# An attention and experts kernel: due times of its host-side planner set anew, and row slots copied by ScalarE block by block

## The chip, the cores and the metric

The kernel runs on one core of a Trainium2 chip. A core has five engines that run their own instruction streams: TensorE (PE; its weight loads are shown apart as PEld), VectorE (DVE), ScalarE (ACT), GpSimd (POOL) and SyncE (SP), which here issues most of the DMA transfers. The metric is the time of one execution on the device in microseconds. Times in the profile are of one profiled execution.

## The reference

Attention on queries that are averaged in twos, and then a layer of eight experts of which each token goes to its two best:

```python
# q, k, v: (4, 8, 1152, 64)
q_pool = q.reshape(B, H, S // 2, 2, D).mean(axis=3)          # 576 queries per head
scores = scale * np.matmul(q_pool, k.transpose(0, 1, 3, 2))
attn = np.exp(scores - scores.max(-1)); attn /= attn.sum(-1)
x = (attn @ v), heads side by side                           # 2304 tokens x 512
logits = x @ w_gate + log1p(exp(x @ w_noise)) * noise        # 8 experts
top2 of the logits, softmax over the two
for e in range(8): out[mask] += weight * (relu(x[mask] @ w1[e]) @ w2[e])   # 512 -> 1024 -> 512
```

## The kernel before

All products run on fp16 or bf16 parts: a float32 operand is split into a high part (ACT, `hi`, L303) and a remainder (DVE, `lo`, L300), and both are multiplied. The attention works through 16 *pairs* (two batch entries of one head), each of them loaded (`qr`, `kr`, `vr`), added in twos (`qs`, L472, on POOL or DVE), split into `qn`, `kn`, `vv`, and transposed by DMA into `qt`, `kt` (L306, issued by SP). For each pair a *maximum pass* of its own (L316 on PE, L324 on ACT, L328 and L346 on DVE) finds each query's largest score; `max_fin` (L353 to L355) writes the maxima into `qn2`, whose transpose `qt2` brings them into the scores. A *tile* of work is then: two chunks of scores on PE (L368, L369), one exponential on ACT (L376, 216 in all), the low half `pl` of the exponential (`p_lo`: one subtraction on DVE, L381, or two on POOL, L384), and the product with the values on PE (L404). Six buffers hold the exponentials, so `pf`, `pl` names repeat every six tiles.

After eight pairs the first half of the tokens is complete, and it is routed while the attention goes on with the other eight pairs: `steps` (L761 and on) is a generator whose pieces compute logits, the two best experts and each token's row slot, mostly on DVE in tiles `rta`, `rua`. Then POOL scatters the token rows into a gather buffer `xg` in DRAM, nine blocks of 128 tokens times two experts, one indirect DMA each (`scatter`, L98). The experts' rows come back transposed as `xe`, and the experts' products (L1047, L1064) fill the rest of the span.

The order of all this in the attention is not written by hand. A class `Plan` runs on the host, while the program is built. Each operation is given to it with its engine (or two to choose from), a cost, a due time (`key`), a latency and the buffers that it takes. `run` keeps a clock for each engine and appends, again and again, the operation that can start first; among those that can start within a limit of the first, the due time counts with 0.01 of its value. So a changed due time, cost or limit can move any instruction on any engine. `DVB` is a handicap of DVE where an operation may go on DVE or POOL, `SLK` a delay of SP's loads; `KEY` and `PAC` are the due time of the first half's routing and the step from piece to piece; `SCW` is a wait between scatters. The 40 writes of zeros into `xg` (L703) and 18 into the output (L559) are SP operations with due times as well. The costs and latencies are the planner's numbers, and not times of the chip.

Of the kernel before, what the change touches and what calls it, by code (L numbers as in the profile page):

```python
# [13 lines left out]
AF = mybir.ActivationFunctionType  # L14
ALU = mybir.AluOpType
# [10 lines left out]
D = 64  # L26
# [6 lines left out]
NB = CAP // P  # L33
FULL = NT
# [25 lines left out]
DVB = 0.3  # L60
SLK = 3.0
LEAD = 20
LATE = 440
KEY, PAC, SCW = 290, 1.4, 1.0
# [48 lines left out]
class Plan:  # L113
# [64 lines left out]
    def run(s):  # L178
        while s.hard or s.holds:
# [39 lines left out]
class Attn:  # L219
# [208 lines left out]
    def pairs(s):  # L428
# [8 lines left out]
        for i in range(NPAIR):  # L437
            b = 27 * i
            x = i == 0
            ahead = (0, -6, -2, 4, 10, 16)[i] if i < 6 else 20  # L440
# [9 lines left out]
            lq.append(op("SP", 2.6, k(60, 95), lambda i=i: s.load_q(i, 1 if i == 0 else 2), lat=3.0,  # L450
# [17 lines left out]
            for p in ((0, 1) if x else (2,)):  # L468
                c = (slice(0, 3), slice(3, NCQ), slice(0, NCQ))[p]
                f = (c.stop - c.start) / NCQ  # L470
                a = op((("POOL", 0.1 + 1.45 * f), ("DVE", 0.07 + 0.74 * f)), 0, k(50, 92) + 8 * p * x,
# [9 lines left out]
                hi = op("ACT", 0.1 + 0.96 * f, k(44, 91) + 8 * p * x, q_hi, deps=[a])  # L481
# [3 lines left out]
                ql.append(op("DVE", 0.07 + 0.6 * f, k(40, 45) + 20 * p * x,  # L485
# [4 lines left out]
            for g in range(3):  # L490
# [17 lines left out]
                red.append(op("DVE", 0.47, k0 + 7 - 8 * soon, lambda i=i, g=g: s.rest_red(i, g), deps=[rest], give=[("R", i, g)]))  # L508
# [10 lines left out]
            lv = op("SP", 0.5, k(16, 40), lambda i=i: s.load_v(i), lat=4.0, take=[("vr", ("vr", i))])  # L519
# [3 lines left out]
            for h, c in enumerate(vs):  # L523
                hi = op("ACT", 0.1 + 0.96 / len(vs), b + 0 + 1 * h, lambda i=i, c=c: s.hi(B["vv", i][:, c, 0:D], B["vr", i][:, c], scale),
# [4 lines left out]
        for u in range(NU):  # L529
# [4 lines left out]
            ex[u] = op("ACT", 0.71, 2 * u + 0.2, lambda u=u: s.exp(u), deps=[sc], take=[("pt", ("pt", u))], give=[("ps", u)])  # L534
# [763 lines left out]
```

## Time and profile before

| what | before |
|---|---|
| median of 3 runs | 862.36 us (862.18 to 863.61) |
| the profiled execution | 858.68 us |
| its span in the profile | 856.9 us |
| mean granted clock of PE | 0.987 |
| busy: PE, DVE, ACT, POOL | 800.1, 522.0, 448.3, 401.0 us |

The span runs from the first to the last instruction that the profiler saw; 1.8 us of the execution lie outside it. A busy time counts an engine's instructions, not their waits. The granted clock is the share of full speed that TensorE was given; full is the upper of its two levels, 2.4 GHz, and 0.50 would be the lower one, 1.2 GHz. The attention reaches to about 485 us, the experts' products from there to about 846 us.

### The profile page before, as it was taken

The numbers are of one execution on the slowest core, as the hardware profiler recorded it, in microseconds if no ns is written. First come the engines' busy times: TensorE is split into PE (matmuls) and PEld (weight loads), VectorE is DVE, ScalarE is ACT, GpSimd is POOL, SyncE is SP. The second block draws the span as 40 slices with busy tenths as digits, with TensorE's granted clock in tenths as the row PEclk, the third lists the DMA queues.
The fourth block names the chain that finished last, engine by engine and source line by source line (L and its number), as shares of the span: only waits on it lengthen the run. The fifth ranks groups of instructions, "written<-read, shape, count | busy, mean of one in ns | idle before, by whom it ended". The sixth has DMA issues, their size and how long they took to land. (4 is left out here: it accounts for less than half of the span.)

```text
span 856.9 us, 21185 instructions
## 1 busy us (share of the span) xinstructions
PE 800.1 (93%) x8694; PEld 532.3 (62%) x8694; DVE 522.0 (61%) x1213; ACT 448.3 (52%) x685; POOL 401.0 (47%) x384
## 2 busy tenths in 40 slices
PE   4889889999999998797999999999999999999994
PEld 1667666777777776576866654565564756647442
DVE  5989888898999899987897231443242332412200
ACT  5777777878788877665554222433232332322310
POOL 4679775998788876578336202111202012030222
PEclk9999999999999999999999999999999999999998
DMA  8999997789896996559658922656629274381243
GB/s 213 202 242 196 233 216 173 180 198 214 189 211 170 197 210 141 144 125 285 168 173 307 228 47 37 177 160 126 154 79 230 62 201 95 84 201 13 31 55 40
DMA packets 214645, 137.21 MB, mean 160 GB/s; under 512 B 148240, under 2 KB 185616, under 8 KB 214544
## 3 DMA queue, kind: packets, MB, share of 16 engines
q1 hardware_dynamic: 205904, 115.74, 55.6%
q0 software_dynamic: 8640, 20.08, 11.6%
q8 instruction: 69, 1.13, 0.5%
q14 instruction: 32, 0.26, 0.1%
HBM read 62.14 MB, written 35.44 MB: 114 GB/s over the span
## 5 line engine op out<-in xcount | busy, mean ns | idle before, releaser
L384 POOL TENSOR_TENSOR pl<-pf 128x384 f16<-128x384 f32 x278 | 274.3, 1018 | 80.3 <-ACT pf L376 60.9
L376 ACT ACTIVATE pf<-pss 128x768 f32<-128x768 f32 x216 | 173.6, 813 | 63.6 <-PE pss L369 56.3
L98 POOL DMA_INDIRECT out_dram<-y,mti x40 | 62.2, 1555 | 308.0 <-ACT y L1069 298.3
L404 PEld LDWEIGHTS <-pf 128*128 128x128 bf16 x2880 | 156.2, 98 | 42.4 <-issue 14.5
L404 PE MATMUL psm<-vv,pf 128*128 128x65 f16 (+1 forms) x2880 | 166.9, 195 | 4.2 <-DVE mx L346 1.2
L404 PE MATMUL psm<-vv,pl 128*128 128x65 f16 (+1 forms) x1440 | 158.1, 193 | 8.1 <-POOL pl L384 4.1
L369 PE MATMUL pss<-qt,kt 66*128 66x384 f16 (+1 forms) x576 | 150.4, 291 | 2.7 <-DMA qt<-qn 2.7
L368 PE MATMUL pss<-qt,kt 128*128 128x384 f16 (+1 forms) x576 | 149.9, 290 | 0.6 <-ACT pf L376 0.5
L1057 DVE SCALAR_TENSOR_TENSOR hl<-pss,hh 128x640 f16<-128x640 f32 (+1 forms) x64 | 46.4, 724 | 162.1 <-ACT hh L1056 162.1
L404 PEld LDWEIGHTS <-pl 128*128 128x128 f16 x1440 | 127.0, 99 | 10.3 <-DVE pl L381 4.6
L1064 PE MATMUL psm<-wl,hh 128*128 128x512 f16 x320 | 121.3, 379 | 0.0
L1064 PE MATMUL psm<-wh,hl 128*128 128x512 f16 x320 | 121.3, 379 | 0.0
L1064 PE MATMUL psm<-wh,hh 128*128 128x512 f16 x320 | 121.3, 379 | 0.0
L1064 PEld LDWEIGHTS <-hh 128*128 128x128 f16 x640 | 62.6, 98 | 73.8
L328 DVE CUSTOM_DVE_ANT_0 rd<-psm,rd 128x512 f32<-128x512 f32 x144 | 97.4, 684 | 14.8 <-ACT rd L324 13.4
L1069 ACT ACTIVATE y<-psm,mg 128x512 f32<-128x512 f32 x40 | 27.4, 688 | 146.6 <-issue 77.3
L1056 ACT ACTIVATE hh<-pss 128x640 f16<-128x640 f32 (+1 forms) x64 | 39.9, 624 | 119.1 <-PE pss L1047 119.1
L324 ACT ACTIVATE rd<-psm 128x512 f32<-128x512 f32 x144 | 85.9, 597 | 14.3 <-PE psm L316 10.8
L381 DVE TENSOR_TENSOR pl<-pf 128x768 f16<-128x768 f32 x77 | 88.0, 1158 | 0.3 <-ACT pf L376 0.2
L316 PE MATMUL psm<-kt,qt 128*128 128x128 f16 (+3 forms) x317 | 74.3, 306 | 11.7 <-DVE mx L328 5.1
L368 PEld LDWEIGHTS <-kt 128*128 128x128 f16 x576 | 56.9, 99 | 22.7 <-issue 10.8
L1047 PE MATMUL pss<-xr,wh 128*128 128x320 f16 x384 | 67.8, 299 | 0.0
(219 smaller groups left out, 1160.3 us busy)
## 6 DMA issues: line engine op xcount, KB each, us to landing
xg<-zt SPq DMA_DIRECT2D x40, 260.0 KB, 4.7
kr<-in_k_dram SPq DMA_DIRECT2D x32, 288.0 KB, 3.6
vr<-in_v_dram SPq DMA_DIRECT2D x16, 576.0 KB, 4.7
kr<-in_moe_w_dram SPq DMA_DIRECT2D x16, 512.0 KB, 5.4
qr<-in_moe_w_dram SPq DMA_DIRECT2D x16, 512.0 KB
kn<-in_moe_w_dram SPq DMA_DIRECT2D x16, 512.0 KB, 4.4
qr<-in_q_dram SPq DMA_DIRECT2D x31, 256.0 KB, 3.5
vr<-in_moe_w_dram SPq DMA_DIRECT2D x14, 512.0 KB, 5.5
```

What stands on the lines that cost most here:

```text
L98: i = nc.gpsimd.indirect_dma_start(out=out, out_offset=bass.IndirectOffsetOnAxis(ap=idx, axis=0), in_=src, in_offset=None, **kw)
L316: s.nc.tensor.matmul(ps[r, o:o + m.shape[1] * P], s.G.buf["qt", i][:, c, r], m, start=True, stop=True)
L324: s.nc.scalar.activation(s.G.buf["rd", i, c], s.G.buf["D", i, c], AF.Relu)
L328: s.nc.vector.tensor_tensor_reduce(out=rd, in0=s.G.buf["S", i, c], in1=rd, scale=1.0, scalar=-3.0e38, op0=ALU.add, op1=ALU.max, accum_out= ...
L368: mm(ps[:, a, o:o + w], kt[:, hh * NK + kc, :], qf[:, q0:q0 + w], start=True, stop=False)
L369: mm(ps[:, a, o:o + w], kt2[0:66, hh * NK + kc, :], qf2[0:66, q0:q0 + w], start=False, stop=True)
L376: s.nc.scalar.activation(s.parts(u)[0], s.G.buf["ps", u][:, :, 0:SG], AF.Exp, scale=0.125 / (IN_SCALE * IN_SCALE))
L381: s.nc.vector.tensor_sub(pl, pf, ph)
L384: s.nc.gpsimd.tensor_sub(pl[:, a], pf[:, a], ph[:, a])
L404: mm(o[:, 0:x], src[:, t % 2, ci * P:ci * P + P], vv[:, hh * NK + kc, a:a + x], start=st, stop=last and src is pl, skip_group_check=True)
L1047: nc.tensor.matmul(ps[:, i, 0:N], w[:, dc, f * P:(f + 1) * P], xT[:, 2 * dc + x, i * N:(i + 1) * N], start=(n == 0), stop=(n == 11))
L1064: s.nc.tensor.matmul(ps, h[:, f, b * P:(b + 1) * P], w[:, f, :], start=(f == 0 and k == 0), stop=(f == 7 and k == 2))
```

## The change

Three kinds of edits. (1) Some forty numbers of the planner change: due times of loads, splits, transposes, zero writes, of the first half's routing and of the first experts, POOL's cost for a `pl` (1.43 to 1.293), the handicap of DVE (0.3 to 0.307) and the limit within which due times are weighed (1.0 to 0.694). (2) In `steps`, for the first half, the row slots are written by DVE as float32 (`sf`), and for each block of 128 tokens ScalarE copies its two slots into the int32 tile `sl` that the scatters read. (3) The two scatters of a block are issued as one piece after that copy, with the wait `SCW` (now 1.424) ahead of each copy, instead of a wait of 1.0 ahead of each scatter. In the changed kernel the lines of the experts stand seven lines lower.

```diff
-DVB = 0.3
-SLK = 3.0
+DVB = 0.307
+SLK = 2.942
-KEY, PAC, SCW = 290, 1.4, 1.0
+KEY, PAC, SCW = 276, 1.434, 1.424
...
-                lim = m + (1.0 if s.soft else cost / 4)
+                lim = m + (0.694 if s.soft else cost / 4)
...
-                lk.append(op("SP", 0.6, k(62, 99) + 2 * h, lambda i=i, h=h: s.load_k(i, h), lat=3.0,
+                lk.append(op("SP", 0.6, k(87.296, 120.229) + 2 * h, lambda i=i, h=h: s.load_k(i, h), lat=3.0,
...
-            pls[u] = op((("POOL", 1.43), ("DVE", 0.87)), 0, 2 * u + 2, lambda eng, u=u: s.p_lo(u, eng), deps=[ex[u]], port=True)
+            pls[u] = op((("POOL", 1.293), ("DVE", 0.87)), 0, 2 * u + 2.533, lambda eng, u=u: s.p_lo(u, eng), deps=[ex[u]], port=True)
...
-            op("SP", 0.6, 20 + 4.7 * x, lambda x=x: R.zero(s.zt, *divmod(x, NB)), deps=[s.set], ready=30.0 + 4.2 * x)
+            op("SP", 0.6, 26.107 + 3.517 * x, lambda x=x: R.zero(s.zt, *divmod(x, NB)), deps=[s.set], ready=30 + 4.765 * x)
...
         sl = T([C, 2], I32)
-        V.scalar_tensor_tensor(sl, idx, float(FULL), rs, op0=ALU.mult, op1=ALU.add)
+        sf = sl if j else T([C, 2])
+        V.scalar_tensor_tensor(sf, idx, float(FULL), rs, op0=ALU.mult, op1=ALU.add)
         mt = (s.tok1 if j == 0 else s.tok2)[:, 3 * gs[0]:3 * gs[0] + C, 2 * DM:].bitcast(F32)
         V.tensor_copy(mt[:, :, 1:5], iw)
-        yield
+        if j:
+            yield
         for c in range(C):
+            if j == 0:
+                yield (SCW, "ACT", 0.25)
+                nc.scalar.activation(sl[:, c], sf[:, c], AF.Copy)
+                yield (0.0, "POOL", 1.1)
             for k in range(2):
                 s.B.scatter(s.xg[:], sl[:, c, k:k + 1], s.xr[j, gs[c // 3]][:, c % 3, :].bitcast(U16), s.group)
-                yield (SCW if j == 0 else 0.0, "POOL", 1.1) if gap else None
+                if j or k == 0:
+                    yield (0.0, "POOL", 1.1) if gap else None
...
-            k0 = LATE + (0, 23, 46)[e]
+            k0 = LATE + (-4.156, 23, 41.252)[e]
```

What the planner makes of it shows in the instructions of an engine in their order. In the rows below a name with a number is one buffer of several, "x2" are two instructions of one kind in a row.

SP at the start of the program, before: `qr`, `kr`, `vr` are the raw loads of queries, keys and values, and L306 are the transposes.

```order
L286 DMA qr<-in_q_dram 128x3x128
L277 DMA kr<-in_k_dram 128x576 x2
L289 DMA qr<-in_q_dram 128x128
L290 DMA qr<-in_q_dram 64x128
L291 DMA qr<-in_q_dram 64x128
L292 DMA qr<-in_q_dram 128x4x128
L306 DMA_TRANSPOSE qt_104<-qn_127 128x3x128
L306 DMA_TRANSPOSE kt_97<-kn 128x9x128 x2
L306 DMA_TRANSPOSE qt_104<-qn_127 128x6x128
L464 DMA kt_0_124<-kt_97 64x1152 x2
L296 DMA vr<-in_v_dram 128x2x576
L277 DMA kr<-in_k_dram 128x576
```

SP at the same place, after the change:

```order
L277 DMA kr<-in_k_dram 128x576 x2
L286 DMA qr<-in_q_dram 128x3x128
L289 DMA qr<-in_q_dram 128x128
L290 DMA qr<-in_q_dram 64x128
L291 DMA qr<-in_q_dram 64x128
L292 DMA qr<-in_q_dram 128x4x128
L306 DMA_TRANSPOSE qt_104<-qn_127 128x3x128
L306 DMA_TRANSPOSE kt_97<-kn 128x9x128 x2
L306 DMA_TRANSPOSE qt_104<-qn_127 128x6x128
L464 DMA kt_0_124<-kt_97 64x1152
L277 DMA kr<-in_k_dram 128x576 x2
L464 DMA kt_0_124<-kt_97 64x1152
```

Pair 0's two key loads now stand ahead of its first query load, and both key loads of pair 1 (the second `kr` row) ahead of the second half of `kt_0_124` and of the values (the row that follows).

POOL from tile 185 on, where the first half's rows are scattered (`xg<-xa,rta`), before. The buffers `pl_113`, `pl_115` to `pl_123` are tiles whose number divided by six leaves 0, 1 to 5; the `pl` here are tiles 185, 186, 188, 190, 197 and 206, and the ones between are DVE's.

```order
L384 TENSOR_TENSOR pl_123<-pf_122 128x384 x2
L98 DMA xg<-xa,rta 18432x1040
L384 TENSOR_TENSOR pl_113<-pf_112 128x384 x2
L98 DMA xg<-xa,rta 18432x1040 x2
L384 TENSOR_TENSOR pl_117<-pf_116 128x384 x2
L98 DMA xg<-xa,rta 18432x1040
L384 TENSOR_TENSOR pl_121<-pf_120 128x384 x2
L98 DMA xg<-xa,rta 18432x1040 x8
L384 TENSOR_TENSOR pl_123<-pf_122 128x384 x2
L98 DMA xg<-xa,rta 18432x1040 x6
L384 TENSOR_TENSOR pl_117<-pf_116 128x384 x2
```

The same place after the change; the `pl` are tiles 181, 187, 190, 192, 202, 206 and 209:

```order
L384 TENSOR_TENSOR pl_115<-pf_114 128x384 x2
L98 DMA xg<-xa,rta 18432x1040 x4
L384 TENSOR_TENSOR pl_115<-pf_114 128x384 x2
L98 DMA xg<-xa,rta 18432x1040 x2
L384 TENSOR_TENSOR pl_121<-pf_120 128x384 x2
L98 DMA xg<-xa,rta 18432x1040 x2
L384 TENSOR_TENSOR pl_113<-pf_112 128x384 x2
L98 DMA xg<-xa,rta 18432x1040 x8
L384 TENSOR_TENSOR pl_121<-pf_120 128x384 x2
L98 DMA xg<-xa,rta 18432x1040 x2
L384 TENSOR_TENSOR pl_117<-pf_116 128x384 x2
L384 TENSOR_TENSOR pl_123<-pf_122 128x384 x2
```

The run of eight scatters stood between tiles 190 and 197 and stands between tiles 192 and 202; the last block's two scatters now follow tile 202.

SP where the transpose that carries pair 4's maxima is issued (`qt_0_108<-qn_0_129`, 128x9x128; `kt_99<-kn` is the key transpose of another pair, `xg<-zt` are zero writes), before:

```order
L292 DMA qr<-in_q_dram 128x4x128
L306 DMA_TRANSPOSE kt_99<-kn 128x9x128 x2
L277 DMA kr<-in_k_dram 128x576 x2
L703 DMA xg<-zt 256x1x520 x3
L306 DMA_TRANSPOSE qt_0_108<-qn_0_129 128x9x128
L464 DMA kt_0_124<-kt_99 64x1152 x2
```

The same transpose after the change:

```order
L292 DMA qr<-in_q_dram 128x4x128
L296 DMA vr<-in_v_dram 128x2x576
L306 DMA_TRANSPOSE kt_99<-kn 128x9x128
L703 DMA xg<-zt 256x1x520
L306 DMA_TRANSPOSE qt_0_108<-qn_0_129 128x9x128
L306 DMA_TRANSPOSE kt_99<-kn 128x9x128
L703 DMA xg<-zt 256x1x520
L277 DMA kr<-in_k_dram 128x576 x2
```

It stood behind both key transposes, two key loads and three zero writes, and now stands behind one key transpose and one zero write.

## Rows read from the trace of the kernel before

**Rows 1.** The page, part 1: busy us (share of the span) xinstructions of each engine.

```profile
PE 800.1 (93%) x8694; PEld 532.3 (62%) x8694; DVE 522.0 (61%) x1213; ACT 448.3 (52%) x685; POOL 401.0 (47%) x384
```

**Rows 2.** Windows of the span: length, busy us of each engine, granted clock, DMA.

```profile
0.00:60.00 60.00, 42.84 (x537) 28.29 (x538) 47.88 (x112) 41.96 (x63) 35.98 (x44) 0.97 0.93 217
60.00:140.00 80.00, 72.29 (x1076) 50.71 (x1074) 70.31 (x177) 60.17 (x96) 60.05 (x65) 0.98 0.97 213
...
320.00:365.00 45.00, 37.85 (x579) 28.84 (x578) 43.68 (x129) 30.51 (x49) 25.45 (x29) 0.96 0.57 144
365.00:425.00 60.00, 53.47 (x1046) 45.12 (x1043) 48.93 (x100) 35.17 (x56) 40.68 (x37) 0.97 0.74 188
...
485.00:846.00 361.00, 361.00 (x2096) 204.87 (x2094) 103.86 (x174) 105.12 (x142) 57.46 (x37) 1.00 0.48 112
```

**Rows 3.** What PE waited for: engine, line, releaser; us in total, times, longest.

```profile
PE pss L316 <- DMA kt<-kn: 9.8, 1, 9.8
PE psm L316 <- DVE mx L328: 8.8, 19, 1.9
PE psm L404 <- POOL pl L384: 4.1, 1, 4.1
PE psm L404 <- DVE pl L381: 3.7, 5, 2.0
...
PE pss L369 <- DMA qt<-qn: 2.7, 4, 1.2
```

**Rows 4.** Windows around two stalls of PE; the clock stands behind POOL's busy time.

```profile
130.00:135.00 5.00, 3.82 (x16) 1.69 (x16) 3.62 (x9) 2.02 (x5) 1.43 (x1) 0.72 0.97 273
395.00:405.00 10.00, 6.59 (x114) 5.26 (x115) 4.21 (x9) 4.51 (x7) 8.29 (x9) 0.83 0.85 316
```

**Rows 5.** Timeline of PE: start, us, instruction, [idle before it <- what ended it].

```profile
131.90 0.32 PE L369 MATMUL pss<-qt,kt 66*128 66x384 f16 x1 [1.18 <-DMA qt<-qn]
...
398.41 0.23 PE L404 MATMUL psm<-vv,pl 128*128 128x65 f16 x1 [4.10 <-POOL pl L384]
```

**Rows 6.** Timeline of the start, 0 to 10 us.

```profile
3.41 0.36 DVE L472 TENSOR_TENSOR qs<-qr 128x192 f32<-128x192 f32 x1 [3.41 <-DMA qr<-in_q_dram]
...
5.78 0.68 ACT L303 ACTIVATE kn<-kr 128x576 f16<-128x576 f32 x1 [0.88 <-DMA kr<-in_k_dram]
...
9.81 0.48 PE L316 MATMUL pss<-kt,qt 128*128 128x128 f16 x3 [9.81 <-DMA kt<-kn]
```

**Rows 7.** Window 320 to 365 us, instructions on tile `rta` (routing) alone.

```profile
320.00:365.00 45.00, 14.05 (x52) 0.51 (x2) 0.00 (x0) 0.96 0.57 144
```

**Rows 8.** Timeline of POOL, 376 to 400 us.

```profile
377.65 1.62 POOL L384 TENSOR_TENSOR pl<-pf 128x384 f16<-128x384 f32 x2
...
382.76 1.92 POOL L98 DMA_INDIRECT xg<-xa,rta  x1 [0.17 <-issue]
...
396.53 0.97 POOL L98 DMA_INDIRECT xg<-xa,rta  x1 [0.30 <-issue]
397.52 1.61 POOL L384 TENSOR_TENSOR pl<-pf 128x384 f16<-128x384 f32 x2
```

**Rows 9.** Line L850: duration ns min/median/max, first and last start, forms.

```profile
L850 ACT ACTIVATE rta<-rta x2: 203/206/208, 365.4 to 449.5; 128x9 f32<-128x9 f32 x1, 128x6 f32<-128x6 f32 x1
```

**Rows 10.** Timeline of DVE, 376 to 385 us.

```profile
377.26 2.83 DVE L381 TENSOR_TENSOR pl<-pf 128x768 f16<-128x768 f32 x1
...
383.75 0.95 DVE L381 TENSOR_TENSOR pl<-pf 128x768 f16<-128x768 f32 x1
```

**Rows 11.** Groups by form: xcount | busy us, mean ns | idle before, releasers.

```profile
L384 POOL TENSOR_TENSOR pl<-pf 128x384 f16<-128x384 f32 x278 | 274.3, 1018 | 80.3 <-ACT pf L376 60.9 <-PE psm L404 10.6 <-PE psm L316 6.5
...
L381 DVE TENSOR_TENSOR pl<-pf 128x768 f16<-128x768 f32 x77 | 88.0, 1158 | 0.3 <-ACT pf L376 0.2
...
L472 POOL TENSOR_TENSOR qs<-qr 128x576 f32<-128x576 f32 x7 | 10.8, 1543 | 18.7 <-DMA qt<-qn 9.5 <-DVE qn L300 9.3
...
L472 DVE TENSOR_TENSOR qs<-qr 128x576 f32<-128x576 f32 x8 | 8.6, 1079 | 0.0
```

More of the change, by code (lines that the diff above doesn't have):

```diff
@@ L439, in pairs @@
             x = i == 0
-            ahead = (0, -6, -2, 4, 10, 16)[i] if i < 6 else 20
+            ahead = (0, -7.066, -1.406, 4, 9.883, 18.027)[i] if i < 6 else 20
             hs = [slice(0, NK), slice(NK, 2 * NK)]
@@ L470, in pairs @@
                 f = (c.stop - c.start) / NCQ
-                a = op((("POOL", 0.1 + 1.45 * f), ("DVE", 0.07 + 0.74 * f)), 0, k(50, 92) + 8 * p * x,
+                a = op((("POOL", 0.1 + 1.45 * f), ("DVE", 0.07 + 0.74 * f)), 0, k(50, 101.104) + 8 * p * x,
                        lambda eng, i=i, c=c: (s.nc.vector if eng == "DVE" else s.nc.gpsimd).tensor_add(
@@ L507, in pairs @@
                           deps=[q, tr[0]] if soon else red, take=[("wide" if soon else "bank", ("R", i, g))])
-                red.append(op("DVE", 0.47, k0 + 7 - 8 * soon, lambda i=i, g=g: s.rest_red(i, g), deps=[rest], give=[("R", i, g)]))
+                red.append(op("DVE", 0.47, k0 + 4.973 - 8 * soon, lambda i=i, g=g: s.rest_red(i, g), deps=[rest], give=[("R", i, g)]))
                 allred += red
@@ L533, in pairs @@
                     give=[(x, i) for i in pr for x in ("kt", "kt2", "qt", "qt2")])
-            ex[u] = op("ACT", 0.71, 2 * u + 0.2, lambda u=u: s.exp(u), deps=[sc], take=[("pt", ("pt", u))], give=[("ps", u)])
-            pls[u] = op((("POOL", 1.43), ("DVE", 0.87)), 0, 2 * u + 2, lambda eng, u=u: s.p_lo(u, eng), deps=[ex[u]], port=True)
+            ex[u] = op("ACT", 0.71, 2 * u + 0.184, lambda u=u: s.exp(u), deps=[sc], take=[("pt", ("pt", u))], give=[("ps", u)])
+            pls[u] = op((("POOL", 1.293), ("DVE", 0.87)), 0, 2 * u + 2.533, lambda eng, u=u: s.p_lo(u, eng), deps=[ex[u]], port=True)
         for n in range(NSEG):
@@ L558, in others @@
         for x in range(NT // P):
-            op("SP", 0.6, 215 + 8 * x, lambda x=x: nc.sync.dma_start(
+            op("SP", 0.6, 216.686 + 8 * x, lambda x=x: nc.sync.dma_start(
                 o[:, x:x + 1].rearrange("p k (h d) -> p (k h) d", h=2), zf[:, None, :].to_broadcast([P, 2, DM // 2])),
-               ready=200.0 + 7 * x)
+               ready=225.102 + 7 * x)
         for c in range(4):
             pool = RAWS[c % 3]
-            ld = op("SP", 0.6, 365 + 8 * c, lambda c=c, pool=pool: F0.load(s.B.flat(pool), c), lat=4.5, take=[(pool, ("fr", c))],
+            ld = op("SP", 0.6, 349.894 + 8 * c, lambda c=c, pool=pool: F0.load(s.B.flat(pool), c), lat=4.5, take=[(pool, ("fr", c))],
                     deps=s.last)
-            hi = op((("DVE", 0.6), ("ACT", 1.06)), 0, 380 + 8 * c, lambda eng, c=c, pool=pool: F0.hi(s.B.flat(pool), c, eng), deps=[ld], port=True)
-            s.f0 = op("DVE", 1.2, 385 + 8 * c, lambda c=c, pool=pool: F0.lo(s.B.flat(pool), c), deps=[hi], port=True, give=[("fr", c)])
+            hi = op((("DVE", 0.6), ("ACT", 1.06)), 0, 458.222 + 8 * c, lambda eng, c=c, pool=pool: F0.hi(s.B.flat(pool), c, eng), deps=[ld], port=True)
+            s.f0 = op("DVE", 1.2, 398.065 + 8 * c, lambda c=c, pool=pool: F0.lo(s.B.flat(pool), c), deps=[hi], port=True, give=[("fr", c)])
         for c in range(4):
@@ L597, in both @@
                 s.open = 2
-                s.route(R.steps(1, (1, 2), R.A, 0.3, s.half[0]), LATE + 8, [], 0.2, True, then=rows, pace=0.35, first=("ACT", 0.25))
-        s.route(R.whole(0), 440, late[0], 0.2, True, then=rows, pace=0.3, first=("PE", 0.4), slot=[("xT", ("xs", 0))])
+                s.route(R.steps(1, (1, 2), R.A, 0.3, s.half[0]), LATE + 8.55, [], 0.2, True, then=rows, pace=0.35, first=("ACT", 0.25))
+        s.route(R.whole(0), 440, late[0], 0.2, True, then=rows, pace=0.316, first=("PE", 0.4), slot=[("xT", ("xs", 0))])
         for x in range(2):
```

22 lines of the change are left out of this document (11 added, 11 removed).

## Prediction

> **What bounds the kernel now.** I read the windows first, then the waits of PE, and only then single stalls. The page gives PE 800.1 us of the 856.9 us span [rows 1], so PE is the bound over the whole, and a change of order can give back only what PE sits idle, plus what its clock loses. The windows split the rest [rows 2]. From 485 to 846 us (the experts) PE is busy all 361.00 us: nothing is to be had there. In the attention, PE's idle time is 17.16 us in 0 to 60, 7.71 in 60 to 140, 7.15 in 320 to 365 and 6.53 in 365 to 425 (each is the stage's length less its PE busy time); in those stages DVE is busy 80, 88, 97 and 82% of the time, so PE mostly waits for what DVE makes.
>
> The waits name it [rows 3]: 9.8 us once for the first transposed keys, 8.8 us in 19 waits for the running maximum on DVE (L328), 4.1 us once for the low half of the exponentials (`pl`) from POOL, 3.7 us in 5 for the same from DVE, and 2.7 us in 4 for transposed queries. A stall can cost twice: after it the granted clock falls below full. Around 131.90 it is 0.72 over 5 us, around 398.41 it is 0.83 over 10 us [rows 4]; 0.28 x 5 and 0.17 x 10 make 1.4 and 1.7 us on top of the stalls of 1.18 and 4.10 us [rows 5].
>
> **The change part by part.** The sum is made against the profiled execution's 858.68 us; the median of the three runs is 3.68 us above it, and I move that difference over unchanged.
>
> *Start.* SP now issues pair 0's two key loads ahead of the first query load. Before, the query piece had landed when DVE added it at 3.41, and the second key half had landed by 5.78 [rows 6]. The transpose of the queries still stands ahead of both key transposes, so it holds them back until the queries are through. If the loads share the queues evenly the query piece lands later by SP's 0.95 us for two issues, my lower end; if it lands only after both key halves, by 5.78 - 3.41 = 2.4 us, the upper end. PE starts at 9.81 on the first key transpose. I take **+1.4 us**, nearer to the lower end, since the loads overlapped before, too.
>
> *Pair 1's maximum pass.* Its two key halves are loaded together, ahead of pair 0's values; before, the second stood behind pair 1's first query transpose. `kn` of its first half is made at tile 6 and not 9 (a tile is one exponential of two key chunks; I number them by counting the exponentials ahead of an instruction in the order), and of its nine maxima five stood at tile 13, where now two come at 12 and three at 13. PE's idle time of 17.16 us less the start's 9.81 leaves 7.35 us in this stage, in which the passes of pairs 0, 1 and 2 lie; only pair 1's moves much. A third of 7.35 is **-2.5 us**; bounds 0 and -7.35.
>
> *Pairs 4 to 6.* The last maximum of pair 4 comes five tiles earlier (48 against 53), of pair 5 four, of pair 6 three, and SP now issues pair 4's `qn2` transpose ahead of one key transpose and two key loads, and behind one zero write, not three. Its scores start at tile 54. That goes for the 1.18 us at 131.90 and the 1.4 us of clock behind it; part of the 2.7 us in four waits can come back at pair 7, which is not earlier. I take **-2 us**; bounds 0 and -(2.7 + 1.4) = -4.1.
>
> *Routing of the first half.* Its 14.05 us of DVE work in 320 to 365 [rows 7] starts five tiles earlier (158 instead of 163), so some of it leaves the stage where DVE is busy 43.68 of 45 us. It goes into tiles 158 to 163, ahead of that stage, where DVE has some room. The stalls behind it are the 3.7 us on DVE's `pl`, longest 2.0. I take that longest one, **-2 us**; bounds 0 and -7.15 (all idle time of the stage).
>
> *Scatters.* Before, POOL ran one, two, one, and then eight scatters in a row, from 382.76 to 396.53 + 0.97 = 397.50, 14.74 us, and only then tile 197's `pl`, for which PE had waited 4.10 us [rows 5, 8]. Seven tiles lie between the `pl` ahead of the run (190) and the one behind it (197); PE takes 53.47 us for the some 30 tiles of the stage, 1.78 us each, so seven cover 12.5 us, and 14.74 + 1.61 us for POOL's `pl` overran them by 3.9, which is the stall. After, the run of eight stands between tiles 192 and 202: ten tiles, 17.8 us, against 16.4. The slack is 1.4 us, so the stall would be gone; but scatters of a block now wait for ScalarE's copy, and the last block in the run has its copy behind the exponential of tile 202. Two scatters at 14.74 / 8 = 1.84 and the pair of 1.61 follow it, 5.3 us, before tile 202's product may start, and PE then has only the two or three tiles in hand (3.6 to 5.3 us). So a stall of 0 to 3 us comes in its place; I take 1. That gives -3.1, and with a quarter of the 1.7 us of clock **-3.5 us**; bounds 0 and -(4.10 + 1.7) = -5.8. Behind the waiting scatter on POOL stands only that `pl`, and PE's L404 waits for it. The row slots are complete at about the same tile (block 8 ends ahead of tile 206 either way), so the gather for the experts isn't late.
>
> *ScalarE's nine copies.* The nearest row is 203 ns for 128 x 9 [rows 9]; nine cost 1.8 us. ACT is busy 35.17 of 60 us in this stage, so they lie in its gaps: **0**; if one stood ahead of an exponential that PE needs, 0.2 us each, 1.8 in all.
>
> *Split of `pl` between DVE and POOL.* The order moves nine tiles from DVE to POOL (POOL 139 to 148) and four query sums (7 to 11). Alone, a tile takes 1.61 us on POOL and 0.95 on DVE [rows 8, 10]; a sum takes 1.543 and 1.079 us in the mean [rows 11]. The two engines together do 9 x 0.66 + 4 x 0.46 = 7.8 us more, while DVE gets free of 9 x 0.95 + 4 x 1.079 = 12.9. DVE is the one that PE waits for, and POOL has 19.95 us idle in 60 to 140, where most moved tiles lie or just ahead. Bounds 0 and +7.8; I take **+1**, near the lower end, because the mean of a tile on DVE, 1.158 [rows 11], is far nearer to 0.95 than to the 2.83 us that one took while POOL worked.
>
> That 2.83 us row began at 377.26, and POOL's pair of 1.62 us lies within it, from 377.65 on [rows 8, 10]: DVE was held, not slow. The Trainium skill, page "SBUF — State Buffer", section "Who interferes with whom", says that an operation of DVE with two inputs in SBUF and one of GpSimd that reads SBUF lock each other out, and whoever issues first wins. By that rule the row agrees, and each moved tile is paid in full by both engines: the sum would hold +7.8 instead of +1. It is the third rival.
>
> *Zero writes and later weights.* The 40 zero writes of the gather buffer and 18 of the output move later by a few us; DMA share in 60 to 140 is 0.97 [rows 2], so this frees queues early on. Cost 0; if they land on the transposes instead, it is part of the 2.7 us above.
>
> Sum: +1.4 - 2.5 - 2 - 2 - 3.5 + 1 = **-7.6 us**, 851.1 by the profiled execution, **855** by the median (862.36 - 7.6 = 854.8).
>
> **The rivals.** (1) *Stalls only change place.* DVE is busy 80 to 97% in every stage where PE waits, so each wait that goes uncovers the next one: tile 202 for 197, pair 7's queries for pair 4's. For it: the 19 waits for L328 are short (8.8 / 19 = 0.46 us) and spread. Against: the two large ones, 4.10 and 1.18 with their clock, have named causes that the order moves. Then the start's +1.4 is left against a gain of 1 to 2: 862. (2) *Nearly all named stalls fall*: +0.95 at the start, -5 of 7.35, -4.1, -4, -5.8 and nothing at the port: -18, 844.5. It asks that DVE's relief of 12.9 us reach PE in each stage; against it, DVE stays over 80% busy in them. (3) *The lock decides, slower.* Place: tiles up to 130 (seven of the nine move there), in stages where DVE and POOL are busy 70.31 and 60.05 of 80 us, 130 us on two engines. It decides once both together with the moved work leave no moment in which one can wait for the other without PE waiting: then +7.8 with +1.4 at the start and only the scatters' -3.5 is +5.7, 868. For it: the 2.83 us row. Against: the two engines have 160 us there. (4) *The copies gate nothing, the due time alone moved the scatters:* same sum, with the slack of 1.4 us and no stall of 1: 854, inside the forecast.
>
> **How the numbers follow.** Forecast, with (4), 849 to 859: 0.52. Stalls change place, 860.5 to 864: 0.15. All fall, 842 to 849: 0.12. Lock, 864.5 to 870: 0.17. The remaining 0.04 lies between the first two. A measurement of this kernel tells 0.2%, 1.7 us, from no change (860.6 to 864.1). Faster takes the forecast, (2) and the gap: 0.69. Same takes most of (1): 0.13. Slower takes (3) and the top of (1): 0.18. The range 846 to 866 leaves out the lower half of (2), 0.06, and two thirds of (3), 0.11.
>
> **What would show it.** Right: PE's first product at 10.7 to 12.2; no 1.9 us wait for L328 near 44; the query wait at pair 4's first score gone and the clock there at 1; the wait for POOL's `pl` near 395 under 3 us; PE idle in 320 to 425 down from 13.7 to about 8. Wrong: a mean of DVE's `pl` above 1.3 us or of POOL's halves above 1.1 (the lock); a new wait for POOL's `pl` at tile 202 of 3 us or more with the clock down (rival 1); waits for transposed queries at pairs 5 to 7.

## The result and the profile after

The changed kernel takes **855.55 us** (median of 20 runs, 848.5 to 862.24) against 862.26 (20 runs, 858.13 to 864.25), or 6.7 us less where 7.6 were forecast. The ratio is 0.9915, 95% interval 0.9897 to 0.9933; it leaves out the run of 862.24, which was slow by its clock, and without it the highest is 857.61. The profiled execution took 855.45 us with a span of 853.7; before's profiled execution lay 3.6 us below its median, so the two traces differ by only 3.2 us. A second profile of each (the first two experiments) is used below wherever one execution could mislead.

The windows of the changed kernel, as in [rows 2], with the one from 425 to 485 added:

```profile
0.00:60.00 60.00, 44.27 (x534) 29.39 (x535) 45.88 (x110) 41.64 (x64) 36.93 (x50) 0.94 0.96 214
60.00:140.00 80.00, 74.08 (x1152) 53.65 (x1148) 69.23 (x181) 63.83 (x102) 71.53 (x79) 1.00 0.91 207
140.00:320.00 180.00, 172.76 (x2892) 131.49 (x2891) 160.06 (x366) 140.90 (x225) 152.29 (x152) 0.99 0.92 197
320.00:365.00 45.00, 41.37 (x658) 31.34 (x655) 41.85 (x127) 32.83 (x54) 32.91 (x35) 0.96 0.52 135
365.00:425.00 60.00, 55.81 (x1028) 47.34 (x1027) 53.27 (x102) 38.81 (x69) 40.45 (x35) 1.00 0.91 222
425.00:485.00 60.00, 53.23 (x377) 35.81 (x375) 37.18 (x146) 23.77 (x45) 24.34 (x22) 1.00 0.77 238
```

and two windows of the kernel before that [rows 2] does not show:

```profile
140.00:320.00 180.00, 176.18 (x2957) 134.43 (x2956) 166.03 (x370) 146.32 (x231) 155.43 (x153) 1.00 0.86 193
425.00:485.00 60.00, 56.44 (x423) 40.08 (x422) 41.28 (x156) 28.40 (x52) 24.41 (x21) 1.00 0.78 235
```

PE's idle time, stage by stage, is 15.73, 5.92, 7.24, 3.63, 4.19 and 6.77 us. Against [rows 2] it fell by 1.79 in 60 to 140, by 3.52 in 320 to 365 and by 2.34 in 365 to 425, and in the first and the last of these the clock is 1.00 where it was 0.98 and 0.97. What the forecast did not hold is in the other rows: 140 to 320 and 425 to 485 are worse, since their idle time was 3.82 and 3.56. The clock of the first stage is 0.94 for 0.97, but the second profile of before has 0.94 there as well. The waits of PE in the changed kernel, as in [rows 3]:

```profile
PE pss L316 <- DMA kt<-kn: 10.9, 1, 10.9
PE psm L316 <- DVE mx L328: 6.2, 15, 1.3
PE pss L1054 <- DVE hl L1104: 5.7, 4, 1.9
PE pss L368 <- ACT pf L376: 4.0, 5, 2.5
...
PE psm L404 <- DVE pl L381: 1.9, 3, 0.8
...
PE pss L369 <- DMA qt<-qn: 0.3, 1, 0.3
```

POOL's 4.1 us is gone from the list, transposed queries fell from 2.7 to 0.3 and DVE's `pl` from 3.7 to 1.9. Exponentials on ACT rose from 0.5 us (1.9 in the second profile of before) to 4.0, and the experts' low half from 2.8 to 5.7. These two in the kernel before, where the experts' line is L1047:

```profile
PE pss L1047 <- DVE hl L1097: 2.8, 3, 1.9
...
PE pss L368 <- ACT pf L376: 0.5, 2, 0.3
```

Since instructions move, a stage between two fixed times mixes work. So I also counted exponentials (L376) in ACT's timeline and took the start of the 42nd, 60th and so on, numbered from 0. Us from the span's start; in brackets the lead (-) or lag (+) against the first profile of before:

| exponential | before | before, second profile | after | after, second profile |
|---|---|---|---|---|
| 42 | 99.7 | 100.3 | 101.8 (+2.1) | 104.9 (+5.2) |
| 60 | 141.5 | 142.2 | 138.5 (-3.0) | 142.1 (+0.6) |
| 162 | 320.3 | 321.0 | 320.0 (-0.3) | 321.7 (+1.4) |
| 186 | 369.7 | 371.2 | 365.8 (-3.9) | 366.0 (-3.7) |
| 210 | 412.9 | 414.3 | 405.1 (-7.8) | 403.8 (-9.1) |
| end of span | 856.9 | 858.3 | 853.7 (-3.2) | 852.8 (-4.1) |

The change from one row to the next is not yet what a step is worth, because the maximum passes move against the exponentials. ACT's part of them (L324) up to exponential 42 and from there to exponential 60, before:

```profile
0.00:99.70 99.70, 20.72 (x35) 0.98 0.95 215
99.70:141.50 41.80, 12.47 (x21) 0.96 0.92 207
```

and after:

```profile
0.00:101.80 101.80, 23.84 (x40) 0.97 0.97 213
101.80:138.50 36.70, 9.97 (x17) 1.00 0.83 207
```

Five more of them stand in the first stretch and four fewer in the second, so the lag at exponential 42 is in part work done ahead. I therefore go by PE's idle time between the same exponentials, in us:

| exponentials | before | before, second profile | after | after, second profile |
|---|---|---|---|---|
| start to 42 | 20.65 | 20.33 | 19.59 | 21.52 |
| 42 to 60 (pair 4's scores) | 4.21 | 4.27 | 2.05 | 2.52 |
| 60 to 162 | 3.82 | 3.82 | 7.24 | 6.53 |
| 162 to 186 (routing) | 7.15 | 6.49 | 3.63 | 3.83 |
| 186 to 210 (scatters) | 6.50 | 6.49 | 3.44 | 2.46 |
| 210 to the end | 14.44 | 14.46 | 18.68 | 18.75 |

Up to exponential 42 neither kernel leads clearly. Pair 4's scores gain about 2 us, the routing about 3, the scatters 3 to 4; 60 to 162 lose about 3, most of it in one wait near 227 us, and the entry into the experts about 4. The rest of the difference is that PE is busy less long with the same 8694 products: 800.1 and 802.4 us before, 799.1 and 797.2 after. Its clock lies below 1.00 in three of the four windows from 60 to 425 us in each profile of before, and in two and in none of them after.

### The profile page after: what moved, and what is told of

The parts are those of the page before. It is cut to its first block, busy times and chain, and to the rows that moved or that the text cites. A ratio compares the mean times of both kernels' runs of the same rounds, so it can differ in the third digit from the quotient of the medians.

```text
span 853.7 us, 21219 instructions
## 1 busy us (share of the span) xinstructions
PE 799.1 (94%) x8694; PEld 531.7 (62%) x8694; DVE 510.2 (60%) x1200; ACT 446.7 (52%) x694; POOL 417.2 (49%) x406
## 5 line engine op out<-in xcount | busy, mean ns | idle before, releaser
L384 POOL TENSOR_TENSOR pl<-pf 128x384 f16<-128x384 f32 x296 | 282.6, 985 | 57.4 <-ACT pf L376 45.2
L376 ACT ACTIVATE pf<-pss 128x768 f32<-128x768 f32 x216 | 173.5, 814 | 60.6 <-PE pss L369 47.5
L369 PE MATMUL pss<-qt,kt 66*128 66x384 f16 (+1 forms) x576 | 151.4, 292 | 0.5 <-DMA qt<-qn 0.3
L324 ACT ACTIVATE rd<-psm 128x512 f32<-128x512 f32 x144 | 85.8, 598 | 14.1 <-PE psm L316 11.9
L381 DVE TENSOR_TENSOR pl<-pf 128x768 f16<-128x768 f32 x68 | 75.5, 1128 | 2.6 <-ACT pf L376 2.5
L369 PEld LDWEIGHTS <-kt 66*128 66x128 f16 x576 | 56.9, 99 | 20.2 <-issue 6.4
L368 PEld LDWEIGHTS <-kt 128*128 128x128 f16 x576 | 57.0, 99 | 19.4 <-issue 6.7
```

The source lines that it names most:

```text
L324: s.nc.scalar.activation(s.G.buf["rd", i, c], s.G.buf["D", i, c], AF.Relu)
L368: mm(ps[:, a, o:o + w], kt[:, hh * NK + kc, :], qf[:, q0:q0 + w], start=True, stop=False)
L369: mm(ps[:, a, o:o + w], kt2[0:66, hh * NK + kc, :], qf2[0:66, q0:q0 + w], start=False, stop=True)
L376: s.nc.scalar.activation(s.parts(u)[0], s.G.buf["ps", u][:, :, 0:SG], AF.Exp, scale=0.125 / (IN_SCALE * IN_SCALE))
L381: s.nc.vector.tensor_sub(pl, pf, ph)
L384: s.nc.gpsimd.tensor_sub(pl[:, a], pf[:, a], ph[:, a])
```

## The experiments

For nine of the kernels the order of all operations that the planner had made was written out as a list of `operation@engine` and replayed with the same buffers, and only that list was edited (in one the copies were also taken out of the code, and the last starts from the order with the experts' old due time). So nothing but the edit moves, which a changed due time can't do here. Names: `k0.0` is a key load of pair 0, `q` a query load, `qs` a query sum, `qm4.2` the transpose of pair 4's maxima, `kt` a key transpose, `z` a zero write, `pl197` a tile's low half.

**Each kernel a second time.** No edit.

> The changed kernel itself once more, for a second profile. In its first profile TensorE waited 2.53 us near 227 us for an exponential that stood on ScalarE behind pair 11's late keys, with a clock of 0.86 behind it, which no step of the prediction holds. If that wait belongs to the order, it stands there again, 2 us or more, and the span is again near 854 us. If it is chance of one execution, it is under 1 us and the span is some 4 us shorter. The start near 10.9 us, the scatters without a wait for POOL and the wait of 1.74 us near 465 us for the experts' low half should repeat in both cases.

> The kernel before once more, for a second profile, since its first came from an execution 3.7 us below the median. The forecast's steps need the same stalls here: 4.1 us for tile 197 behind the scatters and 1.2 us at pair 4's first score, each within a third. The rival view, that the stalls which the steps were priced by are chance, has one of the two under half of that, and others of 1 to 3 us elsewhere; a span of 860 to 862 us would then have to come from those others.

Before took 860.05 us here and showed 4.10 us for tile 197 and 1.29 us at pair 4 again. After took 854.71 us. Most late stalls repeat to some 0.1 us; the wait near 227 us and those near 50 us vary. Timeline of PE in the changed kernel, first profile:

```profile
226.86 0.32 PE L368 MATMUL pss<-qt,kt 128*128 128x384 f16 x1 [2.53 <-ACT pf L376]
...
448.69 0.38 PE L1054 MATMUL pss<-xe,wh 128*128 128x256 f16 x2 [1.69 <-DVE hl L1104]
464.91 1.47 PE L1054 MATMUL pss<-w1x 128*128 128x256 f16 x12 [1.74 <-DVE hl L1104]
```

and second profile:

```profile
51.76 0.48 PE L316 MATMUL psm<-kt,qt 128*128 128x512 f16 x1 [2.18 <-ACT rd L324]
...
229.61 0.32 PE L368 MATMUL pss<-qt,kt 128*128 128x384 f16 x1 [1.70 <-ACT pf L376]
...
397.50 0.20 PE L404 MATMUL psm<-vv,pl 128*128 128x65 f16 x1 [1.02 <-POOL pl L384]
```

The 1.70 us near 227 lies between the two theories' marks. Nor is it settled by the order around it: four kernels below (the first query load first, the copies taken out, pair 4's maxima late, pair 3's load earlier) change nothing around it, and in their traces it is not there. Exponentials 108 to 114, between which it lies, take 9.6 us in each of the four, and 13.9 and 11.9 us in the two profiles of the changed kernel. The last row is tile 202, where the forecast put a stall of 0 to 3 us and took 1.

**The zero writes alone, both ways.** Only `z` (into the gather buffer) and the output's zero writes change place on SP:

```diff
-kt10.0@SP z36@SP kt10.1@SP q11.1@SP z37@SP k11.0@SP k11.1@SP z38@SP kc10.0@SP
+kt10.0@SP kt10.1@SP o1@SP q11.1@SP k11.0@SP k11.1@SP kc10.0@SP
```

(around pair 11's loads, in the changed kernel; `o` is a zero write of the output, `kc` a copy of keys; the last `z` goes back from tile 112 to 97; the other kernel has the reverse)

> The changed kernel with its order kept on every engine; only the zero writes into the gather buffer and the output stand where they stood before among SP's other work. Forecast (zero writes cost nothing, 0): 0 to 1 us against the changed kernel, ratio to the kernel before 0.990 to 0.993. Theory formed after the result: the new spacing puts two zero writes around pair 11's key loads, and the 2.53 us wait with 1.7 us of clock comes of that; then the wait near 227 us goes and the ratio is 0.986 to 0.989. Rival: the later zero writes are what relieved the queues up to 130 us; then waits for transposed queries come back there and the ratio is 0.994 to 0.998.

> The kernel before with its order kept on every engine; only the zero writes stand where the changed kernel has them. Forecast: no change, ratio 0.998 to 1.002. Theory that the new spacing delays key loads after 200 us: a new wait of 2 us or more on TensorE between 200 and 260 us and a ratio of 1.002 to 1.005. Rival, that it relieves the queues early: the waits for transposed queries up to 132 us (2.7 us in 4) fall below 1.5 us and the ratio is 0.995 to 0.998.

After with the old places: 850.48 us, ratio 0.9882 (0.9858 to 0.9905). Before with the new places: 863.55 us, ratio 1.0058 (1.0033 to 1.0083). So the new spacing, costed at 0, costs 0.6% in the kernel before, 5 us, and 0.3% in the changed one, 3 us, where the two intervals still meet. The rival that it relieves the queues is right in its sign and wrong in its time: in the kernel before, PE's waits for transposed queries fall from 2.7 us in 4 at L369 to none with the new places, and in the changed kernel one comes back with the old ones:

```profile
63.84 0.32 PE L369 MATMUL pss<-qt,kt 66*128 66x384 f16 x1 [2.07 <-DMA qt<-qn]
```

With the old places the wait near 227 us is not among those over 0.6 us, but that does not show that the zero writes made it: in the four kernels named above SP issues them in the new places, and the wait is gone there, too. The expected wait between 200 and 260 did not come in the other kernel (0.98 us at 207.76); the time went to many short waits instead. So the runs show that the spacing costs time, and not where. Waits of PE in the kernel before with the new places:

```profile
PE psm L316 <- ACT rd L324: 8.3, 9, 2.0
```

This was 3.3 us in 8 in the first trace of before. What the wait near 227 us is, where it comes, shows on ACT in the changed kernel's first profile: a split of keys that waits for its load stands ahead of the exponential that PE needs.

```profile
225.43 0.68 ACT L303 ACTIVATE kn<-kr 128x576 f16<-128x576 f32 x1 [3.85 <-DMA kr<-in_k_dram]
226.02 0.79 ACT L376 ACTIVATE pf<-pss 128x768 f32<-128x768 f32 x1
```

**The first query load first.**

```diff
-k0.0@SP k0.1@SP q0.0@SP
+q0.0@SP k0.0@SP k0.1@SP
```

ACT's split of the query piece goes back ahead of the first keys with it.

> The changed kernel with its order kept, except that at the very start SP issues the first query load ahead of pair 0's two key loads, and ScalarE splits the query piece ahead of the first keys, as before. Forecast (the start's term, +1.4 us with 0.95 to 2.4): TensorE's first product moves from 10.7 to 10.9 us back to about 9.6, and the time falls by 1 to 2.4 us against the changed kernel, ratio to the kernel before 0.9885 to 0.9905. Rival: the first 60 us have other waits (DVE's maxima) that take the gain, and the clock dip between 20 and 30 us stays; then first product at 9.6 but the 24th exponential no earlier and a ratio of 0.991 to 0.993.

850.45 us, ratio 0.9855 (0.9819 to 0.9891), below the interval of the changed kernel. PE's first product in this kernel, and then two windows of it:

```profile
9.55 0.48 PE L316 MATMUL pss<-kt,qt 128*128 128x128 f16 x3 [9.55 <-DMA kt<-kn]
```

```profile
20.00:30.00 10.00, 9.51 (x111) 6.94 (x111) 8.93 (x18) 8.15 (x13) 3.31 (x4) 0.83 0.96 196
...
50.00:60.00 10.00, 8.98 (x100) 6.30 (x100) 6.00 (x17) 7.68 (x13) 8.31 (x10) 0.83 0.76 186
```

and the same windows of the changed kernel:

```profile
20.00:30.00 10.00, 8.85 (x70) 5.87 (x70) 8.62 (x20) 7.34 (x11) 3.04 (x3) 0.66 0.96 204
...
50.00:60.00 10.00, 9.33 (x137) 7.33 (x137) 8.36 (x21) 8.69 (x15) 8.95 (x10) 1.00 1.06 225
```

The first product comes 1.4 us earlier. The dip of the clock from 20 to 30 us is 0.17 x 10 = 1.7 us smaller, but one as large stands at 50 to 60 instead, and over the first 60 us the clock is 0.94 in both. The trace doesn't carry the lead on, either: the first exponential starts at 21.7 us (22.2 and 22.3 in the changed kernel), the one numbered 24 at 69.1 (66.7 and 70.3) and 42 at 103.0 (101.8 and 104.9). The span is 3 to 4 us shorter (849.7 against 853.7 and 852.8), and 4.3 and 2.3 us lie between exponentials 108 and 114, where the wait near 227 us is absent. So the runs show that this edit is worth 0.6%, 5 us by 0.9915 - 0.9855; that the start is what it gains by is not shown. The rival's sign, an exponential 24 that is no earlier, came; its time did not.

**The old engines below tile 180.** For instance:

```diff
-pl9@POOL qs2.2@POOL pl17@DVE
+pl9@DVE  qs2.2@DVE  pl17@POOL
```

> The changed kernel with its order kept, except that for tiles below 180 each low half and each query sum runs on the engine it had before: 42 operations go from POOL to DVE and 29 from DVE to POOL, nine low halves and four sums more on DVE. The order isn't made for these engines, so waits of its own can come; the busy times tell the split's price. Rival 3 of the prediction (the lock decides): DVE and POOL together are busy some 8 us less and the time falls by 3 us or more, ratio below 0.988. Forecast (+1 for the port, DVE's relief is worth more): DVE busy 10 to 13 us more, POOL 14 to 21 us less, and the time rises by 1 to 6 us, ratio 0.9925 to 0.999. If the split doesn't matter: 0.9895 to 0.992.

858.34 us, ratio 0.9959 (0.9933 to 0.9986): slower than the changed kernel by 0.4%, as was expected, though the intervals meet at 0.9933. Rival 3, which has this kernel faster, is out. Its page, busy times (the profiled execution was one of the longest, 862.36 us):

```profile
PE 803.4 (93%) x8694; PEld 534.0 (62%) x8694; DVE 511.9 (59%) x1213; ACT 447.6 (52%) x694; POOL 398.1 (46%) x384
```

DVE, with nine low halves and four sums more, is busy only 1.7 us more than in the changed kernel (510.2), and POOL 19.1 less (417.2): the two engines save 17 us (14 against the second profile) and PE is later all the same. The expected 10 to 13 us on DVE are there in the moved operations, by groups: low halves and sums take 11.0 us more on DVE and 19.4 less on POOL, 8.4 less together, near the 7.8 of the prediction. The other 9 us are DVE's remaining instructions, which take that much less in this kernel. The order wasn't made for these engines, so part of the 0.4% may be that.

**ScalarE's copies taken out**, with the order kept:

```diff
-        sf = sl if j else T([C, 2])
+        sf = sl
...
-                nc.scalar.activation(sl[:, c], sf[:, c], AF.Copy)
```

> The changed kernel with its order kept, except that DVE writes the first half's row slots as whole numbers again and ScalarE's nine copies are gone; the scatters stand in the same places on POOL and wait for no copy. Forecast (the copy of the last block in the run of eight holds it back to tile 202): TensorE's wait for POOL's low half at tile 202, 0 to 1.0 us in two profiles, falls to 0, the scatters end earlier, and the time falls by 0 to 1 us, ratio 0.990 to 0.992. Rival 4 (the copies gate nothing): scatters at the same times within 0.5 us and the same time. Another rival: without the copies the eight scatters crowd together at tile 192 and delay a low half there; then a wait for POOL of 2 us or more comes and the ratio is 0.994 to 0.997.

856.96 us, ratio 0.9938 (0.991 to 0.9965), which overlaps the changed kernel's interval: the time is not settled. What the copies gate shows on POOL. The first scatter without the copies, and then with them (the changed kernel):

```profile
358.56 1.14 POOL L98 DMA_INDIRECT xg<-xa,rta  x1 [2.59 <-DVE xa L891]
```

```profile
364.31 1.38 POOL L98 DMA_INDIRECT xg<-xa,rta  x1 [5.90 <-ACT rta L897]
...
394.27 0.96 POOL L98 DMA_INDIRECT xg<-xa,rta  x1 [0.30 <-issue]
395.52 3.17 POOL L384 TENSOR_TENSOR pl<-pf 128x384 f16<-128x384 f32 x2 [0.28 <-issue]
```

The first scatter is 5.8 us later with the copies, and 3.4 us later counted from exponential 162 (317.6 without them, 320.0 with): they do hold the first block back. In the run of eight the scatters follow each other at 0.30 us with or without them, so the gate at the last block that the prediction worked out did not bind in this trace. Rival 4 is half right. The early scatters did not help: exponentials 180 to 186 take 17.4 us here, against 14.9 and 13.4 in the changed kernel, with short pauses of PE that the last section returns to. In this trace the copies' hold on the first block is a gain; that is one trace, and the time doesn't settle it.

**Tile 197's low half two scatters earlier, in the kernel before.**

```diff
-r1.62@POOL (scatter) ... r1.63@POOL (scatter) pl197@POOL
+pl197@POOL r1.62@POOL (scatter) ... r1.63@POOL (scatter)
```

> The kernel before with its order kept, except that tile 197's low half stands ahead of the last two of the eight scatters on POOL, not behind them. Forecast (a low half behind a run of scatters is what TensorE waits 4.10 us for, and the clock dip behind it, 1.6 to 1.7 us, comes of the wait): the wait falls to 0.5 to 1.5 us, the dip near 400 us goes, and the time falls by 2.6 to 5 us, ratio 0.994 to 0.997. Rival 1 (stalls only change place): the wait falls, but others of the same size come within 20 us, on the two scatters' later tiles, and the ratio is 0.999 to 1.001.

858.2 us, ratio 0.9949 (0.9923 to 0.9975): this one place is worth 0.5%, or 4.4 us. The low half now starts at 394.11, not at 397.52 [rows 8], POOL is gone from PE's waits, and the window from 395 to 405, 6.59 us busy at a clock of 0.83 in [rows 4], reads

```profile
395.00:405.00 10.00, 9.36 (x182) 7.54 (x180) 9.84 (x14) 6.37 (x10) 8.31 (x7) 1.00 0.86 293
```

Between exponentials 186 and 210 PE idles 4.41 us, where it idled 6.50, so half of the 4.10 us came back in short waits; the dip of the clock is gone.

**Routing alone in the kernel before.** The constants `276, 1.434, 1.424` and the new code of `steps`, with all else as before.

> The kernel before with the first half's routing of the changed kernel alone: its due times (276, 1.434, 1.424) and ScalarE's copies block by block; all other numbers as before. The planner moves other operations too, but none ahead of tile 140. Forecast (routing -2 and scatters -3.5): the 4.10 us wait for POOL's low half is gone or under 1 us, the wait of 1.98 us for DVE's low half near 351 us under 1, and the time falls by 4 to 7 us, ratio 0.992 to 0.9955. Rival: routing alone gives only the scatters' part, 0.995 to 0.998, since the wait near 351 stays. Rival that stalls change place: 0.998 to 1.002.

862.93 us, ratio 1.0001 (0.9975 to 1.0027). Rival 1, for this edit. Waits of PE:

```profile
PE psm L316 <- DVE mx L328: 11.9, 22, 2.0
...
PE psm L404 <- DVE pl L381: 5.5, 7, 2.0
```

The 4.10 us for POOL is down to 1.05, but maxima went from 8.8 to 11.9 us and DVE's low halves from 3.7 to 5.5. (Its profiled execution took 4.5 us more than its median and was 3.9 us behind at exponential 42, ahead of any edit.) Why the routing gives nothing here is not shown. That the old split leaves DVE no room for it is not the reason: between tiles 160 and 180 the two splits differ by one low half, and with the old engines in the changed kernel exponentials 162 to 186 take 43.6 us (45.8 and 44.3 in the changed kernel, 50.6 here, 49.4 before).

**Pair 4's maxima issued late.**

```diff
-qm4.2@SP kt6.1@SP z18@SP k7.0@SP k7.1@SP
+kt6.1@SP z18@SP k7.0@SP k7.1@SP qm4.2@SP
```

> The changed kernel with its order kept, except that SP issues the transpose of pair 4's maxima behind the second key transpose, one zero write and two key loads, as before, and not ahead of them. Forecast (the term for pairs 4 to 6 rests on this place and on the earlier maxima together): a wait of 0.5 to 2 us at pair 4's first score near 128 us with the clock at 0.7 to 0.9 behind it, and 1 to 3.5 us more than the changed kernel, ratio 0.993 to 0.996. Rival: pair 4's maxima are five tiles earlier, which covers the late issue by itself: no wait there, and a ratio of 0.990 to 0.993.

856.61 us, ratio 0.9944 (0.992 to 0.9968), 0.3% above the changed kernel; the intervals overlap, but the trace is plain. PE at pair 4's first score, and the window around it:

```profile
131.22 0.32 PE L369 MATMUL pss<-qt,kt 66*128 66x384 f16 x1 [2.32 <-DMA qt<-qn]
```

```profile
130.00:135.00 5.00, 3.78 (x35) 2.35 (x35) 1.36 (x3) 2.06 (x5) 2.00 (x3) 0.70 1.07 315
```

The wait of before is back, 2.32 us for 1.18 (0.73 to 1.29 in four traces of the old order), with its dip, and PE idles 4.69 us between exponentials 42 and 60: in this trace the place on SP does it, and the earlier maxima alone don't cover it.

**Pair 3's query load earlier**, with pair 2's sum on DVE:

```diff
-qs2.2@POOL ... kc1.0@SP qt2.2@SP z0@SP q3.1@SP
+qs2.2@DVE  ... q3.1@SP kc1.0@SP qt2.2@SP z0@SP
```

> The changed kernel with its order kept, except that pair 2's query sum runs on DVE again, ahead of one maximum, and SP issues pair 3's query load ahead of pair 2's query transpose, not behind it. Theory formed from the traces: the changed kernel issues pair 3's query load near 40 us and not near 33, since it waits for pair 2's sum in the one buffer of raw queries; ScalarE then waits 2 to 4 us for pair 3's sum, the relu behind it comes late, and TensorE waits 1.0 to 2.3 us near 51 us with the clock down behind it. Then here ScalarE's wait near 47 us falls below 1 us, TensorE's near 51 below 0.5, and the time falls by 1 to 4 us, ratio 0.987 to 0.9905. Rival: the late load is covered and the waits near 51 come of other things; same time as the changed kernel, 0.9905 to 0.9925. If delaying pair 2's transpose costs more: above 0.993.

The load that the theory is about, on SP in the trace of before, in the changed kernel, and here:

```profile
32.79 1.15 SPq L289 DMA_DIRECT2D qr<-in_q_dram  x1
```

```profile
39.92 1.29 SPq L289 DMA_DIRECT2D qr<-in_q_dram  x1
```

```profile
36.97 0.38 SPq L289 DMA_DIRECT2D qr<-in_q_dram  x1
```

852.64 us, ratio 0.9899 (0.9857 to 0.9941): not told from the changed kernel. In the trace ACT's wait for pair 3's sum, 2.13 and 4.18 us in the two profiles of the changed kernel, is gone, and so is PE's wait near 51. ACT's second profile of the changed kernel, and this kernel:

```profile
50.06 1.16 ACT L303 ACTIVATE qn<-qs 128x1152 f16<-128x1152 f32 x1 [4.18 <-POOL qs L472]
51.13 0.58 ACT L324 ACTIVATE rd<-psm 128x512 f32<-128x512 f32 x1
```

```profile
48.22 1.16 ACT L303 ACTIVATE qn<-qs 128x1152 f16<-128x1152 f32 x1
```

But a wait of 2.48 us for transposed queries stands at 64.37 here, and exponential 42 starts at 104.4, no earlier than in the changed kernel (101.8 and 104.9): the wait moved. The late load alone doesn't make it, either: with the old zero writes the load is issued at 40.69, and ACT waits 1.01 us.

**Four edits together.** The three above (query load first, old zero writes, pair 3's query load) and

```diff
-            k0 = LATE + (-4.156, 23, 41.252)[e]
+            k0 = LATE + (-4.156, 23, 46)[e]
```

> The changed kernel with four edits together: the first query load first, the zero writes where they stood before, pair 2's sum on DVE with pair 3's query load ahead of pair 2's transpose, and the third expert's first products at their old due time (46 for 41.252). The last should remove the wait of 1.4 to 2.0 us near 461 to 470 us for the experts' low half on DVE. Theory: the parts add, -4 for the queries' start, -3 for the zero writes, -1.5 for the experts, -1 to -3 for pair 3, against the changed kernel: ratio 0.976 to 0.982. Rival: the first two gain by the same early waits and don't add: 0.982 to 0.986.

847.01 us, ratio 0.9843 (0.9806 to 0.988): better than both kernels, and not told from the first edit alone (0.9855), so the rival that early gains don't add is right for time. Its span of 844.9 us is 12.0 below that of before. It leads by 14.0 at exponential 210 (398.9), so the entry into the experts gives back 2.0 us and not 5, and the wait at 465 us is gone:

```profile
PE pss L1054 <- DVE hl L1104: 3.9, 3, 1.9
```

## Why the prediction was right, step by step

The number came out, 855.55 for 855.0, and so did the three steps that carry the sum: pairs 4 to 6, routing and scatters. That the total is so near is luck in part. Losses of about 3 and 4 us that the sum did not hold (60 to 162, and the entry into the experts) stand against PE's shorter busy time, and the spans of the two pairs of profiles differ by 3.2 and 5.5 us, where the medians differ by 6.7.

- **Start, +1.4: right for the first product, open for the time.** It came at 10.94 and 10.71, and between 10.71 and 11.25 in all traces of this order, where the four traces that start as before have 9.41 to 9.85: 1.4 us in the mean. At the first exponential some 0.3 us of it is left. Undoing it gives 0.6%, 5 us by the medians, which the step does not hold; the trace doesn't show where that comes from.
- **Pair 1's maxima, -2.5: the wait went, no gain shows.** The wait of 1.94 us near 44 is gone. But PE idles 20.65 and 20.33 us up to exponential 42 before and 19.59 and 21.52 after, where start and this step together said -1.1; two more traces of the old order have 19.84 and 22.97, so a change of that size can't be seen. The step took only pair 1's pass to move; ACT has done 40 parts of the passes by exponential 42 where it had done 35. Pair 3's query load went from 32.79 to 39.92 us, behind pair 2's sum and transpose, and new waits stand near 51 us (1.02 and 2.18).
- **Pairs 4 to 6, -2: right.** PE's idle time from exponential 42 to 60 fell by 2.2 and 1.8 us, and the clock there rose from 0.96 to 1.00. Issuing the one transpose late brings back 2.32 us of wait and 1.5 of clock (0.30 x 5).
- **Routing, -2, and scatters, -3.5: right in size.** PE's idle time fell by 3.5 and 2.7 us from exponential 162 to 186, and by 3.1 and 4.0 from 186 to 210. Tile 197's place alone is worth 4.4 us in the kernel before, within the bounds 0 to -5.8. The stall at tile 202 that was put at 1 us was 0 and 1.02. That the routing gives this by itself is shown false by the ratio of 1.0001; what else it needs stays open.
- **Port, +1: not borne out as a cost.** Undoing the split made the kernel slower, by 0.4%. Of the nine tiles moved, eight lie below tile 131, not seven, and seven of these below tile 60. Busy times of DVE and POOL, 522.0 and 401.0 before, are 510.2 and 417.2, 4.4 us more together. Groups by form of the changed kernel, against [rows 11]:

```profile
L384 POOL TENSOR_TENSOR pl<-pf 128x384 f16<-128x384 f32 x296 | 282.6, 985 | 57.4 <-ACT pf L376 45.2 <-PE psm L316 4.6 <-PE psm L404 3.9
...
L381 DVE TENSOR_TENSOR pl<-pf 128x768 f16<-128x768 f32 x68 | 75.5, 1128 | 2.6 <-ACT pf L376 2.5
```

Both means fell (1018 to 985 and 1158 to 1128 ns), so a low half was not held up more than before. The Trainium skill, page "SBUF — State Buffer", section "Who interferes with whom", says that a DVE instruction with two SBUF inputs contends with a GpSimd instruction that reads SBUF. The 9 us by which DVE's other instructions took less with the old split are in line with some such price. PE did not pay it, which I put down to POOL's room: PE's waits for POOL are 0 and 1.3 us in the two profiles.

- **Zero writes, 0: failed.** By the runs they cost 3 to 5 us. I had read a lower DMA share early on, and had not asked which transfers they would stand among later. Where they cost it is not shown.
- **Entry into the experts, not in the sum: about +4.** The third expert's earlier due time sets its products among the first's, where PE waits 1.74 us at 465 for a low half that DVE makes behind two weight splits. The run that undoes it gives 2.0 us back after exponential 210, and not 5; it undoes three other things as well, so the 3 us are read from one trace and not separated.

## What to carry to other kernels

Price a low half, a copy or a load that stands behind others in an in-order queue by what is next in that queue: here one place on POOL was worth 4.4 us, one on SP about 2.5 by medians whose intervals overlap, and a whole set of due times for routing nothing by itself. A transfer that nobody waits for can still cost time by its place in the queue: try its old places before calling it free. When operations of several kinds move, compare PE's idle time between the same marks, and see whether the work between the marks is the same. When a forecast's total comes out, look at the stages: here two unpriced losses were covered.

## What was not expected

The two profiles of the changed program agree to some 0.1 us in most late waits but are 3 us apart at exponential 42, where loads land at other times. This is not of the change: four traces of the old order have exponential 42 between 99.7 and 103.6. The wait near 227 us stands in both profiles of the changed kernel and is absent in four others with the same order around it, so two traces do not settle what an edit of that size is worth. Around the scatters PE also shows pauses of about 0.5 us marked "issue", four of them between 362 and 365 us without the copies, for which the profile names no cause; that stays open.
